# Attention sums in two-column-group matmuls, read out of PSUM by VectorE instead of ScalarE

## The chip, the cores and the metric

The kernel runs on one core of one Trainium2 chip. A core has TensorE (matrix products, results in PSUM), VectorE, ScalarE, GpSimd (used here to issue stores) and SyncE (used here to issue loads), and 16 DMA engines between its on-chip memory (SBUF) and the chip's memory. The metric is the device time of one execution in microseconds (us); the time of a kernel is the median of its runs.

## The reference

One decoding step of a transformer block and its gradients. The part that matters here is the attention of one query against a cache of 8192 keys and values, in 32 heads of width 192, all in bf16:

```python
scores = jnp.einsum('bhqd,bhkd->bhqk', q, k) * Dh ** (-0.5)   # one query: 8192 scores a head
p = _softmax(scores, axis=-1)
o = jnp.einsum('bhqk,bhkd->bhqd', p, v)
```

Around it stand a layer norm with modulation from `c`, the projections `wq` and `wo`, and an MLP. The outputs are the block's result and the gradients with respect to the input, both caches, `wq`, `wo`, `w3`, `w4`, `c` and `w_mod`. The gradients of the caches are 201 MB of the output, and the two caches are 201 MB of the input, so the kernel moves 569 MB in all.

## The kernel before, in words

**Stages.** A forward pass goes through heads 0 to 31, a short serial stretch does the MLP forward and backward, and a backward pass goes through the 64 half heads in reverse, reading V again and storing the gradients of K and V. The change is in the forward pass; its lines run from 36 to 531 us of the span.

**Tiles.** A head's K or V, 8192 x 192, is laid out as 128 partitions x 64 positions x 192. It is loaded in halves of 32 positions (`JH`), and worked on in quarters of 16 positions (`JQ`). One position of a quarter, 128 x 192, is what the change's words call a column group. There are five buffers for halves of K (`KB`) and three for halves of V (`VB`).

**What the forward pass makes of a head.** VectorE multiplies each half of K by the query (L333), folds the product (L337), and TensorE sums it by matmuls with the identity (L343); VectorE finishes the scores (L347) and finds the maximum with a detour over TensorE (L551, L555, L561). ScalarE takes the exponentials (L390). Then V is scaled by the exponentials, quarter by quarter, into a tile `vs` (function `g_scale_v`): VectorE does the first `n` positions in one instruction (L403), ScalarE the last `NVA` positions one instruction each (L410). A further column of `vs` holds the exponentials themselves, so that a row of `vs` has `MW` = 193 used columns.

**What is made of `vs`.** For each quarter (`m_quarter`), TensorE multiplies K by `vs` and sums over the positions into `mp` (L425 for 128 of the 192 rows, L430 for the other 64): this is a 192 x 193 matrix that the backward pass uses for the gradient of the query. After that it sums `vs` itself by matmuls with a matrix of ones into `op` (L445): E times V and the sum of E. The matrix of ones has 32 columns, and the four matmuls of four successive positions write to four different groups of 32 partitions of `op`; `pair_sums` later adds the four. When all four quarters of a head are through, `m_out` copies `mp` and `op` to SBUF with ScalarE (L467, L469, L475, L476), and VectorE adds two parts of `mp` (`m_add`, L481), for which it needs L469's result, `mt`.

**Order.** In the forward pass each engine works through its instructions in the order in which the code writes them. The loop runs over heads `i` and mixes three of them: the scores of head `i` (from `x`), the scaling and matmuls of head `i-1` (from `y`), and the last quarter and the reading out of head `i-2` (from `z`). The loads are issued by SyncE, in the order of the code, each waiting until its buffer is free: a half of K is free after L430 of the last quarter that reads it, a half of V when both L403 and L410 have read it (L385 for K, L328 for V). Every second head has extra work for a pair of heads (L497 to L515), and weights are loaded in between (`load_wo`, L203; `load_w`, L197), the latter mostly in every second or fourth head.

The last two heads are handled by straight code behind the loop, with their own shares of the scaling; `m_out` is used there once more for head 29 (`m_out(H1 - 2, ...)`, L706), between the second folding of the scores (L641) and the next product (L638).

The lines that set the order around the change, in the loop's body:

```python
vs0 = scale_v(0, y["v"][0], E4, Ef)
m_quarter(0, y["k"][0], vs0, y["mp"], y["op"])
vs1 = scale_v(1, y["v"][0], E4, Ef)
...
x["v"].append(load_v(i, 1, VB[(2 * i + 1) % NVB]))
if z is not None:
    mt = m_out(i - 2, z["mp"], z["op"], os_)
...
pb = dot_mul(x["k"][1], qh)
if z is not None:
    m_add(i - 2, z["mp"], mt)
```

Of the kernel before, what the change touches and what calls it, by code (L numbers as in the profile page):

```python
# [8 lines left out]
FP32 = mybir.dt.float32  # L9
# [3 lines left out]
AX = mybir.AxisListType  # L13
# [7 lines left out]
def kernel(  # L21
# [27 lines left out]
    P = 128  # L49
    D = A_x.shape[-1]  # L50
    _, HQ, S, DH = A_k_cache.shape
# [5 lines left out]
    JQ = J // 4  # L57
# [11 lines left out]
    MW = DH + 1  # L69
# [5 lines left out]
    V_, A_, T_ = nc.vector, nc.scalar, nc.tensor  # L75
# [24 lines left out]
    ones_bf = const.tile([P, 32], BF16, name="ones_bf")  # L100
# [270 lines left out]

        return H1 - s // 2, (1 - s % 2 if s < 2 else s % 2)

    NVA = (7 * JQ) // 16
    MO = 256
    with tc.tile_pool(name="vs", bufs=3) as vsp, tc.tile_pool(name="ft", bufs=2) as ft, \
            tc.tile_pool(name="psM", bufs=2, space=PS) as psM, tc.tile_pool(name="psO", bufs=2, space=PS) as psO, \
# [34 lines left out]

        def scale_v(q, v, E4, Ef, n=JQ - NVA):
            out = []
            for _ in g_scale_v(q, v, E4, Ef, out, n):
                pass
            return out[0]

        def m_units(q, kb, vs, mp):
            j0 = (q % 2) * JQ  # L420
            z = q == 3

            def main(lo, hi):
                for k in range(lo, hi):
                    T_.matmul(mp[:, 0:MW], lhsT=kb[:, j0 + k, 0:P], rhs=vs[:, k, 0:MW], start=(q == 0 and k == 0), stop=(z and k == JQ - 1), skip_group_check=True)  # L425

            def rest(lo, hi):
                for k in range(lo, hi):
                    p0 = 64 * (k % 2)
                    T_.matmul(mp[p0 : p0 + 64, MO : MO + MW], lhsT=kb[:, j0 + k, P:DH], rhs=vs[:, k, 0:MW], start=False, stop=(z and k >= JQ - 2), skip_group_check=True)  # L430

            return [lambda: main(0, JQ // 2), lambda: main(JQ // 2, JQ), lambda: rest(0, JQ // 2), lambda: rest(JQ // 2, JQ)]
# [7 lines left out]
        def m_quarter(q, kb, vs, mp, op):  # L440
            for f in m_units(q, kb, vs, mp):
                f()
            for k in range(JQ):
                p0 = 32 * (k % 4)
                T_.matmul(op[p0 : p0 + 32, 0:MW], lhsT=ones_bf, rhs=vs[:, k, 0:MW], start=(q == 0 and k < 4), stop=(q == 3 and k >= JQ - 4), skip_group_check=True)  # L445

        def o_rows(h, v2, op, lo=0, hi=J):

# [4 lines left out]
        def os_head(h, os_):  # L453
            t, b = divmod(h, 2)
            if t not in os_:
                os_[t] = ft.tile([P, 2 * DH + 2], FP32, name="osb", bufs=1)
            return os_[t][:, b * DH : (b + 1) * DH], os_[t][:, 2 * DH + b : 2 * DH + b + 1]
# [8 lines left out]
        def mp_out(h, mp):  # L466
            A_.copy(out=M1[:, h, :], in_=mp[:, 0:MW])  # L467
            mt = ft.tile([P, MW], FP32, name="mt", bufs=1)
            A_.copy(out=mt[64:128, :], in_=mp[64:128, MO : MO + MW])  # L469
            return mt  # L470

        def m_out(h, mp, op, os_):
            mt = mp_out(h, mp)
            o, z_h = os_head(h, os_)
            A_.copy(out=o, in_=op[:, 0:DH])  # L475
            A_.copy(out=z_h, in_=op[:, DH:MW])  # L476
            return mt

        def m_add(h, mp, mt):
# [58 lines left out]
        with tc.manual_schedule(engines=ORDER):  # L538
            for i in range(H1):
                x = X.get(i)  # L540
                nx = X[i + 1] = {"k": [], "v": []}
                y = X.get(i - 1) if i > 0 else None
# [13 lines left out]
                if z is not None:  # L556
                    m_quarter(3, z["k"][1], z["vs"], z["mp"], z["op"])
# [8 lines left out]
                    o2 = pair_o(t, po)  # L566
                if y is not None:
                    y["mp"] = psM.tile([P, 512], FP32, name="mp")
                    y["op"] = psO.tile([P, 256], FP32, name="op")
                    vs0 = scale_v(0, y["v"][0], E4, Ef)  # L570
                    m_quarter(0, y["k"][0], vs0, y["mp"], y["op"])
                    vs1 = scale_v(1, y["v"][0], E4, Ef)
# [3 lines that stand above are left out]
# [5 lines left out]
                if y is not None:  # L581
                    m_quarter(1, y["k"][0], vs1, y["mp"], y["op"])
# [9 lines left out]
                if y is not None:  # L592
                    vs = scale_v(2, y["v"][1], E4, Ef)
# [38 lines left out]
            x, y, z = X[H1], X[H1 - 1], X[H1 - 2]  # L632
# [71 lines left out]
            vs0 = new_vs(0)  # L704
            vs_act(vs0, 0, 0, 3)
            mt = m_out(H1 - 2, z["mp"], z["op"], os_)  # L706
            vs_act(vs0, 0, 3, JQ)
            op_y = psO.tile([P, 256], FP32, name="op")
# [207 lines left out]
            for x0, n, pool, tag in ((0, 8, psB, "b"), (8, 7, psM, "mp")):  # L916
                tp = pool.tile([P, 1024], BF16, name="wT_ps", tag=tag)
                wt0.append((x0, n, tp))
                for x in range(x0, x0 + n):
                    b, a = divmod(x, 3)  # L920
# [428 lines left out]
    k, t = 0, TL  # L1349
# [102 lines left out]
    for s in range(NS):  # L1452
# [7 lines left out]
            out=dS4,  # L1460
# [115 lines left out]
```

## Time and profile before

| | us |
|---|---|
| median of three runs | 1389.81 (1385.27, 1389.81, 1391.85) |
| the profiled execution | 1386.39 |
| its span, first to last instruction | 1384.6 |
| TensorE busy | 1154.0 |
| VectorE busy | 1109.2 |
| ScalarE busy | 911.1 |
| DMA | 569.38 MB, mean 411 GB/s |

The profile is one execution, recorded by the hardware. A group of instructions is named by its line in the kernel (L410), its engine, what it writes and what it reads; behind the bar stand its busy time in total, the mean duration of one in ns, the idle time of the engine just before it, and what ended most of that idle time. A window gives the busy time of each engine in a stretch of the span, the clock granted to TensorE (1.00 is full speed), the share of time in which the DMA engines were busy, and the rate. A wait says which engine's line waited for which, with the total in us, the number of times and the longest. The chain of waits follows the work that ended last back to its beginning. Matmuls overlap, so their durations do not add up to busy time. PE is TensorE, PEld its loading of weights, DVE is VectorE, ACT ScalarE, POOL GpSimd, SP SyncE, SPq its queue.

### The profile page before, as it was taken

To read this page: it belongs to the slowest core of one execution; us is meant where nothing else is said; L and a number is where in the kernel's file an instruction comes from. 1 tells how busy PE (TensorE), PEld (TensorE's weight loads), DVE (VectorE), ACT (ScalarE), POOL (GpSimd) and SP (SyncE) were. 2 spreads that over 40 slices of the span, in tenths; PEclk is the share of its full clock that TensorE was granted. 3 is DMA by queue.
4 is the path that set the end of the run, shared out by engine and by line. 5 is a ranking of instruction groups with operands and counts; after the bars stand their busy time and mean duration, and the time that the engine had idled before them with its cause. 6 is when DMAs were issued, how large, how long until landed. Compare 5 with 4: busy or idle time off the path is not lost.

```text
span 1384.6 us, 30509 instructions
## 1 busy us (share of the span) xinstructions
PE 1154.0 (83%) x12712; PEld 733.4 (53%) x12712; DVE 1109.2 (80%) x1455; ACT 911.1 (66%) x2007; POOL 108.6 (8%) x197
## 2 busy tenths in 40 slices
PE   3898989999998989987867977698778886987974
PEld 2777777777777777633323434343334442533421
DVE  4999999999999999986757677686677866876784
ACT  0777777777777778866545656576556665755754
POOL 0000000000000000111100111011101110110011
PEclk8999999999999999765556556565565555655555
DMA  9999999999999999799999999999999999999989
GB/s 383 396 423 425 424 416 423 413 426 418 424 413 425 415 414 380 252 416 424 422 422 425 426 414 426 426 419 425 426 422 425 417 426 384 419 425 426 422 365 378
DMA packets 76889, 569.38 MB, mean 411 GB/s; under 512 B 7439, under 2 KB 25215, under 8 KB 37199
## 3 DMA queue, kind: packets, MB, share of 16 engines
q1 hardware_dynamic: 51594, 342.03, 60.1%
q0 software_dynamic: 24640, 224.89, 38.7%
q8 instruction: 99, 1.62, 0.4%
q10 hardware_dynamic: 516, 0.51, 0.1%
q14 instruction: 40, 0.32, 0.1%
HBM read 340.97 MB, written 226.44 MB: 410 GB/s over the span
## 4 chain that ended last, share of the span: by engine, by line
issue 44%; DVE 25%; DMA 14%; PE 9%; POOL 5%; ACT 2%; POOLq 0%; SPq 0%; ACTq 0%; DVEq 0%
DVE prod L333 10%; DMA KB<-in_A_k_cache_dram 9%; DVE prod L337 5%; DVE vs L403 4%; DMA out_dram<-qs_bc 3%; PE mp L425 2%; POOL out_dram L1414 2%; POOL out_dram L1410 2%; PE half_ps L343 2%; DMA out_dram<-KB 1%; PE mp L430 1%; POOL out_dram L1227 1%; DVE pq L1094 1%; PE dot_ps L1113 1%; DVE S_h L347 1%
## 5 line engine op out<-in xcount | busy, mean ns | idle before, releaser
L1113 PE MATMUL dot_ps<-pq,ident_bf 128*128 128x256 bf16 x1494 | 365.1, 385 | 27.0 <-DVE dP L347 25.5
L410 ACT ACTIVATE vs<-VB,Ef 128x192 bf16<-128x192 bf16 x840 | 303.6, 447 | 0.0
L1125 ACT CAST KB<-dv_ps 128x768 bf16<-128x768 f32 x312 | 241.4, 805 | 83.5 <-PE dv_ps L1124 82.4
L1113 PEld LDWEIGHTS <-ident_bf 128*128 128x128 bf16 x1494 | 147.1, 121 | 172.8 <-issue 137.1
L333 DVE TENSOR_TENSOR prod<-KB,qs_bc 128x6144 bf16<-128x6144 bf16 x62 | 207.9, 3353 | 24.1 <-DMA KB<-in_A_k_cache_dram 16.6
L1124 PE MATMUL dv_ps<-do_r,er_b 1*128 1x192 bf16 x2016 | 220.9, 327 | 4.3 <-ACT KB L1125 2.8
L1129 DVE TENSOR_TENSOR KB<-qh,dS 128x3072 bf16<-128x3072 bf16 x74 | 128.1, 1753 | 95.3 <-DMA out_dram<-KB 76.4
L425 PE MATMUL mp<-vs,KB 128*128 128x193 bf16 x1984 | 188.6, 246 | 4.5 <-ACT vs L410 2.6
L425 PEld LDWEIGHTS <-KB 128*128 128x128 bf16 x1984 | 168.2, 97 | 13.6 <-DMA KB<-in_A_k_cache_dram 5.3
L904 ACT COPY wT<-wT_ps 128x1024 bf16<-128x1024 bf16 x82 | 79.2, 966 | 106.2 <-PE wT_ps L903 105.8
L1124 PEld LDWEIGHTS <-er_b 1*128 1x128 bf16 x2016 | 68.7, 103 | 141.2 <-issue 138.2
L343 PE MATMUL half_ps<-prod,ident_bf 128*128 128x256 bf16 x744 | 95.1, 279 | 44.0 <-DVE prod L337 43.9
L403 DVE TENSOR_TENSOR vs<-VB,E 128x1728 bf16<-128x1728 bf16 x120 | 123.7, 1052 | 0.3 <-ACT vs L410 0.3
L1094 DVE TENSOR_TENSOR pq<-VB,do_r 128x3072 bf16<-128x3072 bf16 x66 | 115.5, 1750 | 0.0
L337 DVE TENSOR_TENSOR prod<-prod 128x3072 bf16<-128x3072 bf16 x62 | 108.7, 1754 | 1.0
L1094 DVE TENSOR_TENSOR pq<-KB,do_r 128x3072 bf16<-128x3072 bf16 x62 | 108.5, 1750 | 0.0
L343 PEld LDWEIGHTS <-ident_bf 128*128 128x128 bf16 x744 | 72.8, 100 | 62.4 <-issue 53.5
L430 PE MATMUL mp<-vs,KB 128*64 128x193 bf16 x1968 | 105.7, 250 | 0.0
L1125 ACT CAST VB<-dv_ps 128x768 bf16<-128x768 f32 x96 | 74.7, 804 | 39.0 <-PE dv_ps L1124 38.7
L1125 ACT CAST qs_bc<-dv_ps 128x768 bf16<-128x768 f32 x104 | 80.1, 805 | 23.7 <-PE dv_ps L1124 23.2
L390 ACT ACTIVATE E<-S_h,negm 128x256 bf16<-128x256 f32 x31 | 15.7, 508 | 114.5 <-DVE negm L561 112.2
L430 PEld LDWEIGHTS <-KB 128*64 128x64 bf16 x1968 | 78.8, 109 | 19.8 <-issue 19.5
(380 smaller groups left out, 1209.4 us busy)
## 6 DMA issues: line engine op xcount, KB each, us to landing
VB<-in_A_v_cache_dram SPq DMA_DIRECT2D x93, 1536.0 KB
out_dram<-KB POOLq DMA_DIRECT2D x74, 1536.0 KB, 17.2
KB<-in_A_k_cache_dram SPq DMA_DIRECT2D x63, 1536.0 KB
KB<-in_A_v_cache_dram SPq DMA_DIRECT2D x29, 1536.0 KB
out_dram<-qs_bc POOLq DMA_DIRECT2D x25, 1536.0 KB, 17.9
out_dram<-VB POOLq DMA_DIRECT2D x25, 1536.0 KB, 17.7
wo_st<-in_A_wo_dram SPq DMA_DIRECT2D x31, 480.0 KB
w_st<-in_A_wq_dram SPq DMA_DIRECT2D x12, 960.0 KB
```

The source lines that it names most:

```text
L333: V_.tensor_tensor(out=prod, in0=src, in1=vec[:, None, :].to_broadcast([P, JH, DH]), op=ALU.mult)
L337: V_.tensor_tensor(out=prod[:, :, 0:HW], in0=prod[:, :, 0:HW], in1=prod[:, :, DH - HW : DH], op=ALU.add)
L343: T_.matmul(ps, lhsT=ident_bf, rhs=prod[:, :, k : k + TF], start=(k == 0), stop=(k == w - TF))
L403: V_.tensor_tensor(out=vs[:, 0:n, 0:DH].rearrange("p j (a b) -> p j a b", b=4), in0=v[:, v0 : v0 + n, :].rearrange("p j (a b) -> p j a b", ...
L410: A_.activation(out=vs[:, k, 0:DH], in_=v[:, v0 + k, :], func=ACT.Copy, scale=Ef[:, j0 + k : j0 + k + 1])
L425: T_.matmul(mp[:, 0:MW], lhsT=kb[:, j0 + k, 0:P], rhs=vs[:, k, 0:MW], start=(q == 0 and k == 0), stop=(z and k == JQ - 1), skip_group_chec ...
L430: T_.matmul(mp[p0 : p0 + 64, MO : MO + MW], lhsT=kb[:, j0 + k, P:DH], rhs=vs[:, k, 0:MW], start=False, stop=(z and k >= JQ - 2), skip_grou ...
L1094: V_.tensor_tensor(out=pq[:, q], in0=v_l[s][:, q * JQ : (q + 1) * JQ, :], in1=do_of(ht(s)[0])[:, None, :].to_broadcast([P, JQ, DH]), op=AL ...
L1113: T_.matmul(ps[:, q * JQ : (q + 1) * JQ, :], lhsT=ident_bf, rhs=pq[:, q, :, k : k + TS], start=(k == 0), stop=(k == w - TS), skip_group_ch ...
L1124: T_.matmul(ps[:, b, k * DH : (k + 1) * DH], lhsT=er[p0 : p0 + 1, 2 * m + k, :], rhs=doh[p0 : p0 + 1, :], start=True, stop=True)
L1125: A_.copy(out=dV4[:, 2 * q : 2 * q + 2, m * PW : (m + 1) * PW], in_=ps[:, :, 0:PW])
L1129: V_.tensor_tensor(out=dK[:, lo:hi, :].rearrange("p j (a b) -> p j a b", b=4), in0=qh.rearrange("p (a b) -> p a b", b=4)[:, None, :, :].to ...
```

## The change

- `NVA` goes from 7 of 16 to 8 of 16: in each quarter ScalarE scales 8 positions, and VectorE's one instruction covers 8 instead of 9.
- The matmuls with ones take two successive positions at a time: 8 in a quarter instead of 16, each with 2 x 193 columns. `op` has two halves, 256 columns apart; even positions are summed into the first and odd ones into the second. It stays in one PSUM bank.
- `m_out` no longer copies `op` with ScalarE: VectorE adds the two halves as it reads them, with a reduction over a pair for the 192 columns of E times V and a second one for the sum of E.

```diff
-    NVA = (7 * JQ) // 16
+    NVA = JQ // 2
@@ m_quarter
-            for k in range(JQ):
-                p0 = 32 * (k % 4)
-                T_.matmul(op[p0 : p0 + 32, 0:MW], lhsT=ones_bf, rhs=vs[:, k, 0:MW], start=(q == 0 and k < 4), stop=(q == 3 and k >= JQ - 4), skip_group_check=True)
+            for k in range(0, JQ, 2):
+                p0 = 32 * (k // 2 % 4)
+                T_.matmul(op[p0 : p0 + 32, :, 0:MW], lhsT=ones_bf, rhs=vs[:, k : k + 2, 0:MW], start=(q == 0 and k < 8), stop=(q == 3 and k >= JQ - 8), skip_group_check=True)
@@ m_out
-            A_.copy(out=o, in_=op[:, 0:DH])
-            A_.copy(out=z_h, in_=op[:, DH:MW])
+            V_.reduce_sum(out=o, in_=op[:, :, 0:DH].rearrange("p a b -> p b a"), axis=AX.X)
+            V_.reduce_sum(out=z_h, in_=op[:, :, DH:MW].rearrange("p a b -> p b a"), axis=AX.X)
@@ in the loop
-                    y["op"] = psO.tile([P, 256], FP32, name="op")
+                    y["op"] = psO.tile([P, 2, 256], FP32, name="op")
```

## The prediction

> **What bounds the kernel now.** I read the windows of the forward pass first (34 to 554 us of the span; only this stage is edited). Columns: busy us of each engine with counts, granted clock, DMA share, GB/s.
>
> ```profile
> 104.00:174.00 70.00, 63.93 (x1011) 53.90 (x1009) 65.40 (x62) 52.52 (x173) 1.09 (x2) 1.00 1.02 425
> 314.00:384.00 70.00, 65.36 (x996) 55.22 (x996) 67.35 (x68) 52.40 (x172) 1.08 (x2) 1.00 1.01 420
> ...
> 310.00:320.00 10.00, 9.92 (x135) 8.48 (x134) 9.88 (x14) 6.75 (x23) 0.00 (x0) 1.00 1.02 431
> 320.00:330.00 10.00, 9.55 (x171) 8.03 (x169) 9.90 (x10) 8.46 (x29) 0.54 (x1) 1.00 1.00 403
> ```
>
> Two things are nearly full: the DMA (share 1.0, 420 of about 430 GB/s) and VectorE (67 of 70 us). ScalarE has a quarter free. The groups of instructions from 100 to 520 us (26 heads) give the prices:
>
> ```profile
> L410 ACT ACTIVATE vs<-VB,Ef 128x192 bf16<-128x192 bf16 x714 | 258.0, 447 | 0.0
> L403 DVE TENSOR_TENSOR vs<-VB,E 128x1728 bf16<-128x1728 bf16 x102 | 105.1, 1052 | 0.3 <-ACT vs L410 0.3
> L445 PE MATMUL op<-vs,ones_bf 128*32 128x193 bf16 x1632 | 52.8, 250 | 0.0
> L347 DVE TENSOR_REDUCE S_h<-half_ps 128x32 f32<-128x256 f32 x50 | 20.9, 419 | 0.4 <-PE half_ps L343 0.4
> L561 DVE TENSOR_REDUCE negm<-mx 128x1 f32<-128x128 f32 x26 | 7.4, 285 | 1.6 <-PE mx L555 1.5
> ```
>
> Then the waits of the same window, SyncE's queue and the engines:
>
> ```profile
> SPq L385 <- PE mp L430: 151.1, 51, 4.5
> SPq L328 <- ACT vs L410: 90.8, 48, 4.2
> ACT E L390 <- DVE negm L561: 86.6, 26, 5.0
> PE half_ps L343 <- DVE prod L337: 27.1, 37, 1.5
> DVE prod L333 <- DMA KB<-in_A_k_cache_dram: 10.3, 8, 2.3
> DVE prod L333 <- ACT vs L410: 3.8, 2, 2.0
> ```
>
> ScalarE waits 3.3 us a head for VectorE, TensorE 1.0 us for VectorE; VectorE waits 0.5 us a head (10.3 + 3.8 over 26), for K loads. So VectorE leads between late K loads. The chain of waits says the same: it runs on VectorE from 281.03 to 332.61 us, then one K load until VectorE starts at 346.15; a cycle of four heads takes 65.1 us, 51.6 of them VectorE's.
>
> ```profile
> 332.61 13.45 DMA KB<-in_A_k_cache_dram
> 346.15 3.36 DVE prod L333
> ```
>
> Last, the timeline, for who releases a V load and where the sums are read out:
>
> ```profile
> 319.69 2.53 ACT L410 ACTIVATE vs<-VB,Ef 128x192 bf16<-128x192 bf16 x7
> 322.24 0.33 SPq L328 DMA_DIRECT2D VB<-in_A_v_cache_dram  x1
> 338.57 0.32 ACT L469 COPY mt<-mp 64x193 f32<-64x193 f32 x1
> 338.91 0.32 ACT L475 COPY osb<-op 128x192 f32<-128x192 f32 x1
> 339.12 0.17 ACT L476 COPY osb<-op 128x1 f32<-128x1 f32 x1
> 339.14 0.35 DVE L481 TENSOR_TENSOR M<-mp,mt 64x193 f32<-64x193 f32 x1
> ```
>
> The V load goes out when ScalarE ends its seven groups (322.22), not when VectorE ends.
>
> **The split 9:7 to 8:8.** VectorE: the same kind of product costs 1052 ns at 1728 elements and 1753 at 3072 (L1129), so 0.522 ns an element, 100 ns a group; four quarters a head: -0.40 us. ScalarE: seven take 2.53 us and one 0.447, so one more each 0.347 us; +1.39 us a head, in a wait of 3.3 us: hidden for ScalarE itself. In every fourth head ScalarE also carries two q projections (L262) and is busy 9.9 of 10 us, but there it waits 1.8 us for L260, which takes up the first two groups' growth. If that cover went, the exponentials of the next head would start late.
>
> **Sums out of PSUM.** The two reductions are on VectorE between the second L403 and the second L333 of a head. From 128 to 256 elements the reduction grows by 134 ns, 1.047 an element: 384 elements give 553 ns, and the one-column sum 153. Back to back an instruction starts 0.08 us before its predecessor's recorded end (two L403 take 2.02, not 2.10): 0.55 us together. Lower end: the 256-element row, 0.42, so 0.41 with the small one. Upper end: the read is strided by 1 KB, which no row shows in PSUM; twice the price per element gives 0.95 + 0.15, less overlap 0.95. I take 0.55, since the strided sum L1003 (20 elements, 0.20 us, in SBUF) stands near the unit-stride L311 (20 elements, 0.175). Their source is complete by then (the last L445 of that head ends 2.7 us earlier). ScalarE loses L475 and L476: 0.27 us from the first's start to the next copy.
> VectorE per head: 0.55 - 0.40 = **+0.15 us** (ends 0.0 and +0.55).
>
> **The wait of L481 on mt.** ScalarE makes mt after two quarters, so 0.69 us later; VectorE arrives 0.55 - 0.20 = 0.35 later. The slack was 0.2 us here (338.89 to about 339.1), 1.0 in the heads with the extra pair work: a stall of 0.14 in every second head, +0.07 a head. Behind L481 stands L337, and TensorE waits for L337 already.
>
> **The op matmuls.** Sixteen take 0.45 us (52.8 us of 1632, and 301.00 to 301.44 between the starts of one group and of the next); eight of twice the columns stream the same columns. Bounds: no gain, if columns decide; half of it, -0.22 us a quarter, if the count does. L425 (193 columns) advances by 90 ns and L343 (256) by 113: columns decide there, so I take -0.05 a quarter, which goes into TensorE's wait for L337: 0 on the path.
> The Trainium skill, page "TensorE: Matmul & The Clock Gate", section on the 56 ns gap, states a floor of about 25 ns from start to start however few the columns. By it the old group is at least 0.40 us and the new one is set by its columns, an estimate of -0.1 us a quarter; by my rows -0.05; the sum is the same either way, because TensorE waits there.
>
> **SyncE's queue and the loads.** The order on the queues of SyncE and GpSimd stays. V loads go out later than the softmax by 0.69 (after two quarters) and by 4 x 0.347 - 0.27 = 1.12 us (after four). Next behind them on the queue stand K loads (325.10 behind 322.24), with 1.9 us or more to spare: not held up. But around 322 the DMA moves 403 GB/s against 431 just before: 0.6 us lost in that window, with few loads in flight. A V load 0.69 us later loses between 0 and 0.69 there, once per cycle; I take 0.35, as it is half empty already.
>
> **The sum.** VectorE +0.22 a head for 30 heads is 6.6 us; in the 13.5 of 65.1 us that belong to the K load it is covered, leaving 5.2; in the first third at 425 GB/s the DMA sets the pace, so about 4.2. V loads: 0.35 x 7 cycles x 0.8 = 1.9. At the end of the forward pass the sums stand once more between L641 and L638, which follow each other without a gap on the chain: +0.5. Total **+6.6 us**. The backward pass runs at DMA share 1.0 and only starts later. On the profiled execution: 1386.4 + 6.6 = 1393.0. That execution lies 3.4 us under the median of the runs shown (1389.81), so for the median: **1396 us**.
>
> **Rivals.**
> Hidden: the K loads set every cycle and VectorE's 0.5 us of waits a head swallow 0.22. For it: DMA share 1.0. Against: the rate sags to 403 once a cycle, so the DMA is not always fed. Time 1390 +-2.
> Faster: halving the count halves L445's 0.45 us. K loads are released by TensorE (151.1 us of SyncE's waits), and each would be released 0.22 to 0.44 us earlier; where TensorE ends last in a third of a head's 0.9 us, 0.9 x 30 / 3 = 9 us less, 1381. It decides from a group under 0.3 us. Against: TensorE's own waits for L337.
> Strided read slow: 0.95 us instead of 0.55, VectorE +0.62 a head, 0.62 x 30 x 0.8 = 15 and 2 for the loads: 1407.
> Clock: the granted clock is 1.00 here and 0.53 from 600 us on, where TensorE is busy 84 of 100 us. Fewer matmuls could cost the full clock in places; the twelve L343 took 2.72 us at the start at 0.5 to 0.8 against 1.47, so one slow set a head, 1.25 less the wait of 1.0, gives 0.25 x 30 = 8 and, with the 6.6, 1404. The same page of the Trainium skill, Part 1, has the clock drop when a window of some 3.4 us is not busy; whether the new groups count as less busy no run here shows.
>
> **How the numbers follow.** 0.5% is 7 us, about what a measurement of this kernel can tell from no change (its runs differ by 6.6). Stretch as summed 0.62, from +2 to +12, cut near its middle by the 7 us: 0.31 same, 0.31 slower. Hidden 0.13: same. Strided or clock 0.12: slower. Faster 0.13. So 0.13 / 0.44 / 0.43. The range takes hidden, the stretch and the strided read, and the edge of the faster case: 1384 to 1408.
>
> **What would show it.** L403 at 0.95 us; L475 and L476 on VectorE at 0.55 and 0.15; L410 x8 with 2.9 us; L445 in 0.40 us or more per eight; VectorE above 68 of 70 us; the DMA's mean in 174 to 454 us below 418; the cycle of four heads at 65.8 to 66.2 us. I am wrong if VectorE's waits for K grow, if the cycle shortens, or if the clock leaves 1.00 before 550 us.

## The result and the profile after

The changed kernel takes 1394.78 us (median of 18 runs, 1389.55 to 1401.63) against 1388.68 us of the kernel before (18 runs, 1384.65 to 1392.78): a ratio of 1.0041, 95% interval 1.0026 to 1.0056, so about 6 us slower. The profiled execution took 1394.6 us with a span of 1392.8 us.

First the groups of the changed kernel from 100 to 520 us (columns as before: count, busy us, mean ns, idle before):

```profile
L410 ACT ACTIVATE vs<-VB,Ef 128x192 bf16<-128x192 bf16 x800 | 287.3, 443 | 0.0
L403 DVE TENSOR_TENSOR vs<-VB,E 128x1536 bf16<-128x1536 bf16 x100 | 93.1, 952 | 0.0
L445 PE MATMUL op<-vs,ones_bf 128*32 128x386 bf16 x800 | 51.5, 334 | 0.0
L475 DVE TENSOR_REDUCE osb<-op 128x192 f32<-128x384 f32 x25 | 13.8, 554 | 0.4
L476 DVE TENSOR_REDUCE osb<-op 128x1 f32<-128x2 f32 x25 | 3.7, 149 | 0.0
L481 DVE TENSOR_TENSOR M<-mp,mt 64x193 f32<-64x193 f32 x25 | 8.8, 352 | 2.7 <-ACT mt L469 2.3
```

Every price of the new instructions is as estimated: 952 ns, 554 ns, 149 ns, and a wait of L481 for `mt` of 2.3 us in 13 of 25 heads (0.09 us a head). TensorE's sixteen matmuls of 193 columns in 52.8 us per 1632 are now eight of 386 in 51.5 us per 800: 0.515 us a quarter where it was 0.518.

Some lines from the timeline of one head show the steps (start, us, engine, line, count). First the kernel before, where the exponentials of this head start at 397.41, then the changed one, where they start at 399.31:

```profile
397.41 0.51 ACT L390 ACTIVATE E<-S_h,negm 128x256 bf16<-128x256 f32 x1 [3.78 <-DVE negm L561]
...
403.51 0.33 SPq L328 DMA_DIRECT2D VB<-in_A_v_cache_dram  x1
```

```profile
399.31 0.51 ACT L390 ACTIVATE E<-S_h,negm 128x256 bf16<-128x256 f32 x1 [2.77 <-DVE negm L561]
...
402.60 0.55 DVE L475 TENSOR_REDUCE osb<-op 128x192 f32<-128x384 f32 x1
...
403.21 2.87 ACT L410 ACTIVATE vs<-VB,Ef 128x192 bf16<-128x192 bf16 x8
...
406.11 0.33 SPq L328 DMA_DIRECT2D VB<-in_A_v_cache_dram  x1
...
406.65 0.35 DVE L481 TENSOR_TENSOR M<-mp,mt 64x193 f32<-64x193 f32 x1 [0.17 <-ACT mt L469]
```

The load of V goes out 6.80 us after the start of the exponentials; in the kernel before it was 6.11 us in every head (397.41 to 403.51 here). The second load of V in a head goes out at 13.3 to 13.7 us, where it was 12.2 to 12.4 (in the heads without extra work). The loads of K hardly move: in these two heads they go out 0.34 and 8.91 us after the exponentials in the kernel before, 0.54 and 8.91 us in the changed one.

Next, where the time went. From the first to the last exponentials of the loop, the forward pass takes 499.9 us instead of 493.0; what comes behind takes 857.7 instead of 856.5. Within the forward pass, the first 16 steps from head to head take 265.5 us (265.6 before), the last 14 take 234.4 (227.3 before). So in this execution all of the loss lies in the last 14 heads. That is not a fixed place: the kernel e6 below, whose forward pass is as long (499.8 us), has 268.4 and 231.4 us. The windows of the last third, first of the kernel before, then of the changed one (busy us of PE, PEld, DVE, ACT and POOL with counts, granted clock, DMA share, GB/s):

```profile
384.00:454.00 70.00, 64.54 (x999) 54.23 (x997) 67.89 (x79) 53.31 (x175) 1.08 (x2) 1.00 1.01 419
454.00:524.00 70.00, 64.62 (x1003) 54.27 (x1000) 66.89 (x64) 54.80 (x182) 2.69 (x5) 1.00 1.00 410
```

```profile
384.00:454.00 70.00, 62.96 (x841) 50.45 (x838) 66.41 (x90) 55.90 (x177) 1.08 (x2) 1.00 0.99 404
454.00:524.00 70.00, 62.02 (x819) 49.32 (x817) 64.77 (x70) 56.54 (x179) 2.15 (x4) 1.00 0.99 395
```

The reader is to see three things. VectorE is not busier than before but less (66.41 for 67.89, 64.77 for 66.89), although it has more work: it waits. The granted clock stays at 1.00. And the rate of the transfers falls by 15 GB/s in each of the last two windows. In bytes, over 384 to 524 us, the kernel before and the changed one:

```profile
DMA packets 7008, 58.01 MB, mean 414 GB/s; under 512 B 736, under 2 KB 2048, under 8 KB 2624
```

```profile
DMA packets 6820, 55.98 MB, mean 400 GB/s; under 512 B 712, under 2 KB 2024, under 8 KB 2600
```

2.03 MB less in the same 140 us; at 420 GB/s that is 4.8 us of transfer. The lost bytes do not say by themselves what cost them: a kernel that is slower for another reason moves less there too (e2 below). The chain of waits of the changed kernel there:

```profile
399.85 14.02 DMA KB<-in_A_k_cache_dram
...
435.94 2.78 ACT vs L410 x8
...
461.83 12.33 DMA w_st<-in_A_wq_dram
...
477.34 13.04 DMA KB<-in_A_k_cache_dram
```

From 384 us on, the kernel before has two transfers on its chain (K loads of 12.25 and 11.94 us); the changed one has three, the K loads longer, and ScalarE's scalings, which were on no such chain, stand in it too. The waits of L333 in this third that end in a late transfer (2.6 us of K loads, and 2.5 us at 413.97, which the table of waits puts down to L410 but the chain to the K load of 399.85) come to 5.1 us, where they were 2.4.

### The profile page after: what moved, and what is told of

Its sections match the earlier page's. It is cut to its first block, busy times and chain, and to the rows that moved or that the text cites. A ratio compares the mean times of both kernels' runs of the same rounds, so it can differ in the third digit from the quotient of the medians.

```text
span 1392.8 us, 28709 instructions
## 1 busy us (share of the span) xinstructions
PE 1180.3 (85%) x11752; PEld 722.3 (52%) x11752; DVE 1113.7 (80%) x1515; ACT 947.5 (68%) x2067; POOL 108.8 (8%) x197
## 4 chain that ended last, share of the span: by engine, by line
issue 42%; DVE 22%; DMA 16%; PE 9%; POOL 5%; ACT 4%; SPq 0%; POOLq 0%; ACTq 0%; DVEq 0%
DMA KB<-in_A_k_cache_dram 9%; DVE prod L333 8%; DVE prod L337 4%; DMA out_dram<-KB 3%; DMA out_dram<-qs_bc 2%; PE mp L425 2%; ACT vs L410 2%; DVE vs L403 2%; POOL out_dram L1414 2%; PE half_ps L343 2%; POOL out_dram L1410 2%; DVE pq L1094 1%; PE mp L430 1%; POOL out_dram L1227 1%; DMA w_st<-in_A_wq_dram 1%
## 5 line engine op out<-in xcount | busy, mean ns | idle before, releaser
L1113 PE MATMUL dot_ps<-pq,ident_bf 128*128 128x256 bf16 x1494 | 379.1, 397 | 29.3 <-DVE dP L347 28.2
L410 ACT ACTIVATE vs<-VB,Ef 128x192 bf16<-128x192 bf16 x960 | 344.8, 443 | 0.0
L1113 PEld LDWEIGHTS <-ident_bf 128*128 128x128 bf16 x1494 | 150.6, 124 | 183.3 <-issue 144.7
L1124 PE MATMUL dv_ps<-do_r,er_b 1*128 1x192 bf16 x2016 | 227.5, 338 | 2.8 <-ACT KB L1125 2.1
L333 DVE TENSOR_TENSOR prod<-KB,qs_bc 128x6144 bf16<-128x6144 bf16 x62 | 207.7, 3350 | 24.6 <-DMA KB<-in_A_k_cache_dram 17.1
L343 PE MATMUL half_ps<-prod,ident_bf 128*128 128x256 bf16 x744 | 95.0, 279 | 53.9 <-DVE prod L337 53.8
L343 PEld LDWEIGHTS <-ident_bf 128*128 128x128 bf16 x744 | 73.3, 100 | 81.9 <-issue 73.0
L403 DVE TENSOR_TENSOR vs<-VB,E 128x1536 bf16<-128x1536 bf16 x120 | 111.7, 952 | 0.0
L337 DVE TENSOR_TENSOR prod<-prod 128x3072 bf16<-128x3072 bf16 x62 | 108.7, 1754 | 1.0
L347 DVE TENSOR_REDUCE dP<-dot_ps 128x32 f32<-128x512 f32 x64 | 43.9, 686 | 46.7 <-PE dot_ps L1113 46.2
```

Source lines behind the costliest of these rows:

```text
L333: V_.tensor_tensor(out=prod, in0=src, in1=vec[:, None, :].to_broadcast([P, JH, DH]), op=ALU.mult)
L337: V_.tensor_tensor(out=prod[:, :, 0:HW], in0=prod[:, :, 0:HW], in1=prod[:, :, DH - HW : DH], op=ALU.add)
L343: T_.matmul(ps, lhsT=ident_bf, rhs=prod[:, :, k : k + TF], start=(k == 0), stop=(k == w - TF))
L403: V_.tensor_tensor(out=vs[:, 0:n, 0:DH].rearrange("p j (a b) -> p j a b", b=4), in0=v[:, v0 : v0 + n, :].rearrange("p j (a b) -> p j a b", ...
L410: A_.activation(out=vs[:, k, 0:DH], in_=v[:, v0 + k, :], func=ACT.Copy, scale=Ef[:, j0 + k : j0 + k + 1])
L1113: T_.matmul(ps[:, q * JQ : (q + 1) * JQ, :], lhsT=ident_bf, rhs=pq[:, q, :, k : k + TS], start=(k == 0), stop=(k == w - TS), skip_group_ch ...
```

## The experiments

Two theories. **The V theory**: ScalarE releases the V buffers later (0.69 us after two quarters, 1.1 to 1.3 after four), the loads go out later, and the transfers, which are the limit, fall behind. **The VectorE theory**: VectorE's own 0.22 us a head (sums, split, wait for `mt`; 0.25 and 0.28 in the trace) set the pace. Beside them the rival from the matmuls' count. "Own pace" below is the time from head to head where VectorE waits for no load; it comes in a long and a short form, 16.14 and 15.37 us in the kernel before. All times are medians of 8 to 12 runs, with the ratio to the kernel before on the same chip.

**The split alone (e1_split_only).** The kernel before with

```diff
-    NVA = (7 * JQ) // 16
+    NVA = JQ // 2
```

> The split 8:8 alone: ScalarE still copies the sums out of PSUM, and the sixteen one-column-group matmuls stay. Theory VectorE (the time follows what VectorE does and waits for in a head, at the rate that the change showed, 6.1 us for +0.25 us a head, so 24 us per us a head): VectorE -0.40 us a head by two rows (1052 to 952 ns, four times); but ScalarE makes mt 0.69 us later, VectorE comes to L481 0.2 us earlier, and with 0.2 us of slack before it stalls 0.7 us in every second head, +0.35 a head; sum -0.05 a head, -1 us, between -4 and +3. Rival V loads (the time follows how late ScalarE frees the halves of V): they go out 0.7 and 1.4 us later than before, at least as late as in the changed kernel, so +6 or more.

Measured: 1391.49 us, ratio 1.0021 (1.0002 to 1.0040), 2.9 us slower. VectorE has less to do, and its own pace shows it in the long form: 15.74 us, 0.40 less. In the short form it is 15.64 us or more, at least 0.27 longer, because L481 now waits for `mt`. V loads go out at 6.80 and about 13.8 us after the exponentials. The waits of the split-only kernel, 100 to 520 us:

```profile
DVE prod L333 <- DMA KB<-in_A_k_cache_dram: 17.0, 12, 3.2
DVE M L481 <- ACT mt L469: 7.1, 12, 0.7
```

The 0.4 us a head by which VectorE's own work is shorter went into waits for K (17.0 us, 10.3 before) and for `mt`, and somewhat more than that was lost. The 2.9 us (interval 0.3 to 5.6) lie at the upper end of what the VectorE theory allowed (-4 to +3) and are half of what the V theory asked for (+6 or more). This run alone decides between neither.

**The sums alone (e2_sums_only).** The changed kernel with `NVA` back at 7:

```diff
-    NVA = JQ // 2
+    NVA = (7 * JQ) // 16
```

> The two-column-group matmuls and VectorE's sums out of PSUM, with ScalarE left at 7 of 16. Theory VectorE: +0.55 us a head (0.554 + 0.149 less two overlaps), no stall on mt, 24 us per us: +13, between +9 and +16. Rival V loads: the second of the two V loads of a head goes out 0.27 us earlier than before, so 0 or a little less. A rival that blames the longer matmuls would show here and in the next kernel alike.

Measured: 1395.22 us, ratio 1.0050 (1.0034 to 1.0066), 6.7 us slower, half of what was expected. Own pace 16.79 and 15.90 us: VectorE's sums cost 0.65 and 0.53 us a head in full. Over 30 heads that is up to 19.5 us, of which a third reached the total; waits for K loads fell from 10.3 to 5.0 us. The first V load stays at 6.11 us; the second goes out at 12.77 us in the long form (12.39 before) and at 11.90 in the short one (12.17 before). So VectorE's time counts too, at about a third of its length. The bytes from 384 to 524 us fall here as well (58.01 MB before, 55.98 in the changed kernel):

```profile
DMA packets 6900, 56.87 MB, mean 406 GB/s; under 512 B 720, under 2 KB 2032, under 8 KB 2608
```

**The matmuls alone (e3_matmuls_only).** Eight matmuls of two groups, `NVA` 7, and ScalarE copies only the first half of `op`, so that the odd positions are left out of the sums:

```diff
-            V_.reduce_sum(out=o, in_=op[:, :, 0:DH].rearrange("p a b -> p b a"), axis=AX.X)
-            V_.reduce_sum(out=z_h, in_=op[:, :, DH:MW].rearrange("p a b -> p b a"), axis=AX.X)
+            A_.copy(out=o, in_=op[:, 0, 0:DH])
+            A_.copy(out=z_h, in_=op[:, 0, DH:MW])
```

> Only the matmuls of two column groups; ScalarE stays at 7 of 16 and copies only the first of the two halves, so the odd positions are left out of the sums. Theory VectorE: nothing of VectorE or of ScalarE changes, 0, within 2 us. If halving the number of matmuls helps TensorE, up to -9; if two-group matmuls are slower, above 0: then part of the 6 us is theirs.

Measured: 1387.08 us, ratio 0.9988 (0.9973 to 1.0004); own pace 16.14 and 15.37 as before, forward pass 492.3 us for 493.0. The halved count brings nothing that can be told from no change.

**V later, VectorE's work unchanged (e4_later_v), and its control (e5_before_madd).** In the kernel before, ScalarE does the last scaling of each quarter twice, so that it releases V later; `m_add` is put behind the folding L337, so that VectorE need not wait for a later `mt`. The control has only the second edit:

```diff
@@ e4 alone
-                A_.activation(out=vs[:, k, 0:DH], ...)
+                for _ in range(2 if k == JQ - 1 else 1):
+                    A_.activation(out=vs[:, k, 0:DH], ...)
@@ e4 and e5
                 pb = dot_mul(x["k"][1], qh)
+                dot_half(pb)
                 if z is not None:
                     m_add(i - 2, z["mp"], mt)
-                dot_half(pb)
```

> The kernel before, with the last scaling of each quarter done twice by ScalarE (so eight instructions for seven positions) and the addition of mt (L481) moved behind the folding (L337), so that a late mt stalls nothing. V loads go out 0.7 and 1.4 us later than before; VectorE's work is as before. Theory V loads: +3 to +6 us. Theory VectorE: 0, or some tenths of the lost 0.2 us of slack: between -2 and +2.

> The kernel before with L481 behind L337 and nothing else: the control for e4. Nothing is late in it, so 0, within 2 us, by either theory. If it is slower by some us, that part of e4's 7.6 us belongs to the moved addition and not to the later V loads.

Measured: 1396.21 us, ratio 1.0066 (1.0034 to 1.0098), for the later V; 1387.64 us, 0.9986 (0.9968 to 1.0004), for the control. Some 0.5 us more of ScalarE's work a quarter cost about 8 us against the kernel before and 11 against the control, though VectorE had nothing more to do. That is above what the V theory gave, and a price far from my 1.9 us. The delay was larger than meant, though, and larger than in the changed kernel: the V loads go out at 7.08 and 14.1 to 14.4 us after the exponentials, 1.0 and 2.0 us later than in the control (6.11 and 12.2 to 12.4). VectorE's own pace is that of the control, 16.26 and 15.49 us for 16.27 and 15.49. (The profiled execution of the later V took 1411.4 us and is not like the median, so its waits and windows are not used.)

**Both parts again, without VectorE's wait (e6_after_madd, e7_split_madd).** The changed kernel, and the split alone, each with the same move of `m_add`.

> The changed kernel with the addition into M2 (L481) put behind the halving L337, so that VectorE no longer waits for ScalarE's copy mt (2.3 us over 25 heads in the changed kernel's trace). Theory that VectorE's own work and waits set the pace: 0.09 us less a head, at 0.6 to 1 of it over 30 heads 2 to 3 us less than the changed kernel, 1392 to 1393 us. Theory that the later loads of V do it: the V buffers come free as late as in the changed kernel, so 1394 to 1396 us. Either way the row L481 <- ACT mt should be gone.

> The kernel before with 8 of 16 column groups on ScalarE, its own sums and matmuls, and the addition L481 put behind L337: VectorE has 0.40 us less a head and no wait for mt, while ScalarE releases the V buffers later, as in the split-only kernel (1391.5 us). Theory that VectorE sets the pace: 0.40 us x 30 heads x 0.6 to 1 less than before, 1377 to 1382 us. Theory that the later loads of V set it: no gain, 1390 to 1393 us, and waits of L333 for K loads that take up what VectorE gives. The head at VectorE's own pace should be about 15.85 and 15.1 us (16.14 and 15.37 before) under both.

Measured: 1394.34 us (1.0035, 1.0017 to 1.0053) for the changed kernel so moved. The wait of L481 is gone, but the move itself makes the long form longer (16.52 for 16.39; in the control 16.27 for 16.14), so the run does not price the wait; it shows only that its end brings nothing. For the split: 1391.62 us (1.0003, 0.9976 to 1.0030), own pace 15.86 and 15.1 as expected, some 10 us or more above the VectorE theory's 1377 to 1382. VectorE now has 0.4 us a head less and no wait for `mt`, and the kernel is no faster: the time went into waits for K loads (16.1 us, 10.3 before) and for TensorE's sums (L347 for L343, 4.2 us, 0.4 before), which itself waits longer for weights (6.5 us, 2.1 before).

**V loads in quarters (e8_after_vq, e9_before_vq, e10_split_madd_vq).** Each V load is cut in two, and the first half of it goes out when the first of its two quarters is scaled: about 3 us earlier for half of the bytes. In the changed kernel, in the kernel before, and in the split with the moved `m_add`:

```diff
+    def load_vq(h, t, v, q):
+        nc.sync.dma_start(out=v[:, q * JQ : (q + 1) * JQ, :], in_=V_hd[h][:, t * JH + q * JQ : t * JH + (q + 1) * JQ, :])
...
                     vs = scale_v(2, y["v"][1], E4, Ef)
+                v0b = load_vq(i + 1, 0, VB[(2 * i + 2) % NVB], 0)
...
-                nx["v"].append(load_v(i + 1, 0, VB[(2 * i + 2) % NVB]))
+                nx["v"].append(load_vq(i + 1, 0, v0b, 1))
```

and in the same way for the half `(i, 1)`.

> The changed kernel, with each V load of the loop cut into two quarters: the first goes out when the first of the two quarters is scaled, some 2.9 us earlier than the whole load does now, the second when the whole load does now. VectorE, ScalarE and TensorE do what they do in the changed kernel. Theory V loads: the DMA is fed again when it runs short, 3 to 6 us less than the changed kernel, 0 to +3 against the kernel before. Theory VectorE: as the changed kernel, +6, between +4 and +8.

> The same cut of the V loads in the kernel before. Theory V loads: the rate sags in it too (403 against 431 GB/s once in a cycle), so 1 to 4 us less. Theory VectorE: 0, within 2 us, since VectorE does the same.

> The split 8:8 with ScalarE's copies (e1), L481 behind L337 so that a late mt stalls nothing, and the V loads cut into quarters. VectorE does 0.40 us a head less than before, and nothing that was found to make up for it is left. If VectorE and the V loads are the two causes, this is faster than the kernel before by 3 to 8 us; if the K loads set the pace as soon as VectorE is faster, 0 to -2.

Measured: 1395.99 us (1.0044, 1.0025 to 1.0062), 1392.23 us (1.0018, 1.0001 to 1.0036) and 1392.79 us (1.0019, 1.0000 to 1.0039). None shows the gain that earlier V loads should bring, and the waits say why; the kernel before with quarters, 100 to 520 us:

```profile
PE q_ps L260 <- DMA w_st<-in_A_wq_dram: 9.9, 6, 2.9
DVE S_h L351 <- PE half_ps L347: 10.7, 6, 5.1
DVE prod L337 <- DMA KB<-in_A_k_cache_dram: 2.6, 3, 1.3
```

(L337 and L347 are the lines L333 and L343 of the other kernels, four lines further down.) The waits for K fell from 10.3 to 2.6 us; that fits an earlier V, but VectorE also came later to them. For the first quarter of the next V load now stands ahead of the weights in SyncE's order: the loads of the weights go out 1.8 us later (11.67 us after the exponentials for 9.83), TensorE waits for them up to 2.9 us at a time (9.9 us in all, 2.1 in the kernel before), and behind it VectorE. Behind the longest of these waits TensorE is also slower:

```profile
210.96 1.75 PE L260 MATMUL q_ps<-w_st,ha_bf 128*128 128x384 bf16 x5 [2.94 <-DMA w_st<-in_A_wq_dram]
```

The same five matmuls take 0.97 us in the kernel before, and the granted clock of the window from 174 to 244 us is 0.95, where it is 1.00 in the kernels before and after. Single heads take 20 to 22 us. These three runs mix three effects (V earlier, weights later, a lower clock) and settle nothing; they led to the next.

**V loads in quarters behind the weights (e11_after_vq2, e12_split_madd_vq2).** The same, with one line further down:

```diff
                 if i % 4 == 0 and mb < NMB:
                     nb = min(CW // P, NMB - mb)
                     wch = load_w(wm_v, mb * P, (mb + nb) * P)
...
+                v0b = load_vq(i + 1, 0, VB[(2 * i + 2) % NVB], 0)
                 if y is not None:
                     m_quarter(2, y["k"][1], vs, y["mp"], y["op"])
```

> The changed kernel with each V load cut into two quarter loads, the first issued as soon as the first quarter of the buffer is scaled, but here behind the loads of w and wo in SyncE's order, so that these are not delayed. Theory that the later V loads cost most of the 6 us: half of V's bytes go out 3 us or more earlier than in the changed kernel, so 1389 to 1391 us, with the waits of L333 for K below 5 us between 100 and 520 us of the span (10.9 us in the changed kernel). Theory that VectorE's 0.22 us a head does it: 1394 to 1396 us. Waits of L260 for w should be as in the changed kernel; if they are not, this run settles nothing.

> 8 of 16 column groups on ScalarE, the sums and matmuls of the kernel before, the addition L481 behind L337 and V loads in quarters behind w and wo: VectorE has 0.40 us less a head and V's bytes go out earlier. If VectorE's pace and the later V loads are the two causes, both are cured here: 1378 to 1384 us, faster than both kernels. If the transfers themselves hold the loop (420 GB/s between 100 and 520 us of the span and no more to be had), VectorE's gain turns into waits for K and the time is 1387 to 1391 us.

Measured: 1388.87 us (0.9997, 0.9980 to 1.0013) for the changed kernel with it. That is 6 us less than the changed kernel (and 5.5 less than e6 on the same chip), and its loss is gone. The waits, windows and bytes of that kernel (waits from 100 to 520 us, bytes from 384 to 524):

```profile
DVE prod L337 <- DMA KB<-in_A_k_cache_dram: 7.6, 6, 1.9
```

```profile
384.00:454.00 70.00, 64.22 (x870) 51.60 (x868) 68.35 (x88) 57.68 (x182) 1.08 (x2) 1.00 1.01 416
454.00:524.00 70.00, 63.17 (x846) 50.30 (x844) 66.57 (x72) 58.60 (x186) 2.69 (x5) 1.00 1.00 407
```

```profile
DMA packets 9414, 57.66 MB, mean 412 GB/s; under 512 B 1003, under 2 KB 2315, under 8 KB 7224
```

The last two windows are back at 416 and 407 GB/s (404 and 395 in the changed kernel), the 140 us move 57.66 MB for 55.98, and VectorE is busy 68.35 us again. No wait of L260 for the weights is left in the table, and the clock is 1.00 in all six windows. VectorE's own pace is 16.39 and 15.65 us, exactly that of the changed kernel: its 0.25 us a head are all still there, and the forward pass takes 493.6 us all the same (493.0 before, 499.9 changed). The waits for K were expected under 5 us and are 7.6; the time was expected at 1389 to 1391.

The other one, with VectorE's pace at 15.86 us, takes 1388.54 us (0.9991, 0.9974 to 1.0009). Against the run just told, VectorE has half a us less to do in a head, some 16 us over 30 heads, and the kernels are 0.3 us apart. In its place VectorE waits for K:

```profile
DVE prod L337 <- DMA KB<-in_A_k_cache_dram: 15.7, 12, 2.5
DVE prod L337 <- ACT vs L414: 4.0, 2, 2.1
```

So the 1378 to 1384 us of the two causes cured together fell. What holds the loop at about 492 us then is, as far as these runs go, the transfers: 421 GB/s from 104 to 384 us in both of these kernels and in the kernel before, at a DMA share of 1.01 to 1.02. No version that was run is measurably faster than the kernel before.

## Why the prediction was right

**The total.** 1396 us was said, 1394.78 came; +6.6 us on the profiled execution, +6.1 between the medians (0.41%). That lies inside the 0.5% that were called the limit, in the case "same", which had nearly the same chance as "slower".

**The prices of the instructions held**: VectorE's split -0.40 us a head (measured in e1's own pace), the sums 0.554 and 0.149 us for 0.553 and 0.153, the stall of L481 0.09 us a head for 0.07, ScalarE's eight in 2.87 us for 2.9, the V load 0.69 us later as said and the second 1.1 to 1.3 for 1.12. The own pace of VectorE grew by 0.25 and 0.28 us for 0.22.

**The two terms of the sum were missized, in opposite directions.** "VectorE 4.2 us" was too much: by e2, where VectorE alone is slower, 0.65 us a head cost 6.7 us, a third; a third of 0.25 us over 30 heads is 2.6. "V loads 1.9 us" was too little: e1, where VectorE gains 0.4 us in the long heads and loses some 0.3 in the short ones, is 2.9 us slower, and e4, where only the V loads are later, by more than in the changed kernel, costs 8 us. With 2.9 for the V loads and 2.6 for VectorE the sum is 5.5, near the 6.1 measured. This division is rough: e1's interval alone runs from 0.3 to 5.6 us. Nor do the two simply add, as e11 shows: with the V loads earlier, VectorE's part costs nothing that can be seen in the total. That the total came out within half a microsecond was luck, since one error covered the other. What failed is the step that took 51.6 of 65.1 us as VectorE's on the chain, and so VectorE's time as four fifths of the price. The reading was off to begin with: the last 6.6 of these 51.6 us, from this line to the K load at 332.61, are TensorE's.

```profile
325.97 1.47 PE half_ps L343 x12
```

And the rule behind it does not hold: VectorE leads between two late loads, but whatever it gains or loses there mostly goes into or comes out of the next wait for a load. And the V load's price was taken from one window once a cycle (0 to 0.69); the lag is met in every head, twice. For e4 such a bound is too low: 1.0 us in each of 7 cycles is 7 us, and the price was 8 or more. For the changed kernel the runs do not decide it: 7 times 0.69 is 4.8 us, and 3.5 are left beside VectorE's 2.6.

**What was to be seen.** L445 at 0.40 us or more per eight, and the DMA's mean below 418 from 174 to 454 us (425, 417, 417, 404: 416), held. "VectorE above 68 of 70 us" failed (66.3 on average, 66.7 before), and so did the cycle of 65.8 to 66.2 us: in the profiled execution the loss is nothing in the first 16 heads and 0.5 us a head in the last 14. "I am wrong if VectorE's waits for K grow" came true in that last third (2.4 to 5.1 us), hardly in the whole window (10.3 to 10.9): the total was right by a wrong division.

**The rivals.** Hidden (1390): fell, the loss is real, though the mechanism, loads that set the cycles, is nearer to what the runs show than my own sum. Faster by the matmuls' count: fell in e3. From the start of a group to that of the next it is still 0.46 us (338.01 to 338.47), far above the 0.3 from which it was to decide. Eight of 386 columns in that time are 57 ns each, sixteen of 193 were 28 ns: the columns decide. The Trainium skill's floor of about 25 ns from start to start (page "TensorE: Matmul & The Clock Gate", section on the 56 ns gap) agrees with that: neither form reaches it, and so the count had nothing to give. Strided read: fell, 554 ns for 384 elements in pairs 1 KB apart is the price per element of the unit-stride rows (L1003, on which the choice leaned, takes 0.189 us and not 0.20, which changes nothing). Clock: fell, 1.00 in all six windows of the changed kernel.

**Open.** Whether the kernel before with V quarters behind the weights would itself be faster was not run. In e11 the first half of each V load goes out at 3.9 and 10.4 to 11.2 us after the exponentials, earlier than in the kernel before (6.11 and 12.2 to 12.4); so it is not known how much of e11's 6 us undoes the lag and how much is a gain of its own, and the division of the 6 us between VectorE and the V loads stays open with it. Nor is it shown why the first 16 heads bear the same lag without loss in the changed kernel's execution and lose 2.8 us in e6's.

## What to carry to other kernels

Where the DMA is at its limit and one engine is nearly full, do not price a change of that engine by its busy time alone, but also by what it does to the times at which buffers come free: here 0.4 us a head less on VectorE made nothing faster and 0.65 more cost a third of it, while releasing V 1.0 and 2.0 us later, with VectorE's pace unchanged, cost 8 us or more. Work moved to an engine "with a quarter of its time free" need not be free if that engine's last instruction releases a buffer. And where a load is cut so that its first part goes out sooner, look at what stands behind it in the issuing queue: in the changed kernel the same cut ahead of the weights brought nothing, behind them 6 us.

## What the runs showed of the hardware

- A VectorE reduction over pairs that lie 1 KB apart in PSUM costs no more per element than one over neighbours: 554 ns for 384 elements, where the rows at 128 and 256 elements (285 and 419 ns), carried on, give 553.
- Half as many matmuls with twice the columns into groups of 32 partitions take the same time, 0.515 us a quarter for 0.518.
- Behind a wait of TensorE of 2.94 us (e9) five matmuls of 384 columns took 1.75 us for 0.97, with a granted clock of 0.95 in the 70 us around them.
- Two halves of a load in place of one showed no cost to the transfers: 421 GB/s from 104 to 384 us in e11, as in the kernel before. The Trainium skill, page "Perfetto Trace Analysis", section "DMA Optimizations", has it that cutting transfers may let some start sooner, and names idle DMA engines as the case; here it went with 6 us less although the DMA share of the changed kernel was 0.99 to 1.01.
